# Attention and a mixture of experts on one core: first-row scores of two heads from a tile of their own

## The chip, the cores and the metric

One core of a Trainium2 chip runs the whole program. TensorE (PE in the views; PEld is its weight load), VectorE (DVE), ScalarE (ACT) and GpSimd (POOL) each work through a fixed list of instructions in order and wait for each other by semaphores; SyncE (SP) issues the DMAs. The metric is device time in microseconds (us) of one launch, the median of several runs.

## The reference

```
scores = scale * np.matmul(q, k.transpose(0, 1, 3, 2))      # (4, 8, 576, 64) each
bias = -(cum[:, :, :, None] - cum[:, :, None, :])           # cum: cumsum of max(s, 0)
scores = np.where(causal, -1e9, scores + np.minimum(bias, 0.0))
attn = softmax(scores);  x = attn @ v                       # -> (2304, 512)
for e in range(4):
    h = np.maximum(x @ w1[e], 0.0)                          # 512 -> 1024
    out += p[:, e:e + 1] * (h @ w2[e])
```

Everything is float32. Where a product needs more than one pass, the kernel splits an operand into a rounded part ("hi", type F32R) and the remainder ("lo") and adds products of the parts.

## The kernel before, in words

**Stages.** First comes attention over 32 heads. While it runs, TensorE also works through the first expert (group by group of token tiles, lines L888 and L901), which fills the places where attention has nothing ready. What is left of the first expert then runs alone, while GpSimd and the DMAs prepare the operands of the last stage. The last stage, experts 1 to 3, is a seven-product scheme (L1189 first layer, L1199 second layer).

**Order.** For the attention stage the class `Sched` plays the program on the host with cost estimates for each task: a task has the engines that may do it, a priority, the buffers that it takes and gives back, and the tasks that it depends on. The order in which this play starts the tasks is the order of the instructions on each engine of the chip. TensorE's filler is taken whenever no attention task is ready by the play's own clock. After that the chip's engines simply follow their lists.

**A visit.** The loop over `VISITS` handles one head at a time. The first eight heads come first, in two halves each; visits 16 to 39 are the other 24 heads, each with all 576 query rows at once, and the two heads of a neighbouring pair follow each other. For a head of these 24, q and k arrive as one `raw` tile [128, 576] (rows 0 to 63 are q, 64 to 127 are k, transposed). ACT or POOL makes the hi part, DVE or POOL the lo part, in the tile `AB`. Three DMAs build `KK` from it (L654 to L656; the last copies rows of the cumulated bias out of the DRAM tile `ce_d`), and two DMAs fill the second half of `AB` (L660, L661). A score tile is then two accumulating matmuls (L696): 128 rows deep, for the hi parts of q with hi and lo of k, and 68 deep, for the lo part of q and the bias rows. Behind it come a masked row minimum on DVE (L707), the exponential on ACT (L715), the normalisation (L430/L432), transposes on TensorE (L742) and the product with v (L793).

**The first 64 rows.** Rows 0 to 63 of a head see only 64 keys. The function `pair_rows` does them for two neighbouring heads in one softmax tile of 128 rows: head one in rows 0 to 63, head two in rows 64 to 127. Before the change its scores are four matmuls (L546), two for each head, each with 64 columns. Their weights are 128 columns of that head's `AB`, read from 64 columns further left for the second head, so that it lands in the lower rows; `AB` has 64 columns more for that, which GpSimd clears (L361). The first of the pair's visits so keeps its `AB` and `KK` until the second visit has its own. The v rows of the pair come in two small DMAs (L533) into `vraw0`. Later, L584 multiplies the pair's probabilities with its v.

**The weights' staging tiles.** `stage` is two tiles [128, 1024] through which the eight weight blocks of the first expert are loaded and split, early in attention.

Of the kernel before, what the change touches and what calls it, by code (L numbers as in the profile page):

```python
# [61 lines left out]
def t_act(n, psum=True):  # L62
    return n / 1.2 + (55 if psum else 95)
# [258 lines left out]

def body(ctx, tc, qk, vp, s, dp, w1, w1s, w2, w2s, out):
    nc = tc.nc
# [31 lines left out]

    def AB_raw(j, dt=F32R):
        fresh = late.get(tok["AB", j], (None, None))[0] != dt
        t = slot(tok["AB", j], [P, 64 + 2 * S], dt, apool)
        if fresh and dt == F32R:  # L360
            nc.gpsimd.memset(t[:, 0:64].bitcast(F32), 0.0)  # L361
        return t

    def AB(j, dt=F32R):
        return AB_raw(j, dt)[:, 64:].rearrange("p (x n) -> p x n", x=2)

# [36 lines left out]
    make("xh", 1, [P, 2, S])  # L403
    make("stage", 2, [P, 1024])
    make("osb", 2, [P, DM])
    make("mx", 8, [P, 2])
    make("sm", 8, [P, 1])
    make("vraw0", 1, [P, D])
    make("V0", 2, [P, P], F32R)
# [118 lines left out]

    def pair_rows(j, h, base, ready, last):
# [5 lines left out]
        v_hi = sch.add({"ACT": t_act(64, False), "POOL": (t_pool_hi(64), D2)}, lambda e: hi(e, tok["V0", k][:, 0:64], tok["vraw0", k]), [ldv],  # L535
                       prio=base - PV, take=[("V0", k)], seq="V0")
        v_lo = sch.add({"DVE": (t_dve(64), D7), "POOL": (t_pool2(64), 0)}, lambda e: sub(e, tok["V0", k][:, 64:P], tok["vraw0", k], tok["V0", k][:, 0:64].bitcast(F32)),
                       [v_hi], prio=base - PV, give=[("vraw0", k)])
# [58 lines left out]
    pair_deps = {}  # L597
    qk_before, last_before = [], None
    x_done = {}
# [4 lines left out]
    for j, (h, ms) in enumerate(VISITS):  # L604
# [3 lines left out]
        ext = rows(ms[-1])[1]  # L608
        q0 = rows(ms[0])[0]
        nb = ms[-1] + 1  # L610
        first = j < NH
# [30 lines left out]
        else:  # L642
            if pq:
                qk_ready = [ld, ldc]
            else:
                qk_hi = sch.add({"ACT": t_act(ext, False), "POOL": (t_pool_hi(ext), D2)}, lambda e, j=j, ext=ext: hi(
                    e, AB(j)[:, 0, 0:ext], tok["raw", j][:, 0:ext]), [ld], prio=base - PQ, take=[("AB", j)], seq="AB")
                qk_lo = sch.add({"DVE": (t_dve(ext), D7), "POOL": (t_pool2(ext), 0)}, lambda e, j=j, ext=ext: sub(
                    e, AB(j)[:, 1, 0:ext], tok["raw", j][:, 0:ext], AB(j)[:, 0, 0:ext].bitcast(F32)),
                    [qk_hi], prio=base - PQ, give=[("raw", j)])  # L650
                qk_lo.both = True

                def f(e, j=j, h=h, ext=ext):
# [5 lines left out]
                def f(e, j=j, h=h, ext=ext, q0=q0):  # L659
                    nc.sync.dma_start(out=AB(j)[64:128, 0, q0:ext].bitcast(F32), in_=AB(j)[0:64, 0, q0:ext].bitcast(F32))  # L660
                    nc.sync.dma_start(out=AB(j)[64:68, 1, q0:ext].bitcast(F32), in_=ced[h, 0:4, q0:ext])  # L661
                q_dma = sch.add({"SP": 1100}, f, [k_dma], prio=base - 1600, xfer=256 * (ext - q0))
                qk_ready = [k_dma, q_dma]
# [9 lines left out]
        last_q = None  # L673
        joint = ms == tuple(range(NC))
        if joint and o:
            pair_rows(j, h, base, qk_before + qk_ready, last_before)
        for m in ms[1:] if joint else ms:
# [7 lines left out]
            for pi, (j0, j1) in enumerate(pieces):  # L685
                lastp = pi == len(pieces) - 1

                def f(e, j=j, a=a, j0=j0, j1=j1, c=c, pi=pi, ext=ext, pq=pq, h=h):
# [8 lines left out]
                qt = sch.add({"PE": (t_pe4(j1 - j0) if pq else 2 * t_pe(j1 - j0))}, f, qk_ready + [last_q], prio=pr + pi, take=[("S", (c, pi))],  # L697
                             give=([("AB", j)] if pq else [("AB", j), ("KK", j)] if o or not joint else []) if lastp and m == ms[-1] else [])
                last_q = qt
# [163 lines left out]
    for which in (1, 2):  # L863
        for i in range(4):
            pr = (W1 if which == 1 else W2) + i
            k = (which, i)
            ld = sch.add({"SP": 500}, lambda e, k=k: load_w(0, k[0], k[1], tok["stage", k]), prio=pr - 5500 + WS, take=[("stage", k)], xfer=524288)
            n, lo = 1024 // WH, None
            for x in range(WH):
                c0, c1 = x * n, x * n + n  # L870
                hd = sch.add({"ACT": (t_act(n, False), DWA), "POOL": (t_pool_hi(n), DWQ)}, lambda e, k=k, c0=c0, c1=c1: hi(
                    e, w_tiles(*k)[0][:, c0:c1], tok["stage", k][:, c0:c1]), [ld, lo], prio=pr)
                lo = sch.add({"DVE": (t_dve(n), DWL), "POOL": (t_pool2(n), DWP)}, lambda e, k=k, c0=c0, c1=c1: sub(
                    e, w_tiles(*k)[1][:, c0:c1], tok["stage", k][:, c0:c1], w_tiles(*k)[0][:, c0:c1].bitcast(F32)),
                    [hd], prio=pr, give=[("stage", k)] if x == WH - 1 else [])
# [516 lines left out]
```

## Time and profile before

| | |
|---|---|
| median of 3 runs | 925.06 us (924.97 to 925.24) |
| profiled execution, own time | 925.23 us |
| its span, first to last instruction | 923.4 us |
| busy PE, PEld, DVE, ACT, POOL | 99%, 95%, 75%, 49%, 53% of the span |
| granted TensorE clock | 1.00 throughout |

The profile's times count from the span's start. The program spends 1.8 us of its own time outside the span. A busy figure is the time in which an engine has at least one instruction under way; matmuls overlap, so the pace of TensorE is read from the distance of starts and not from durations.

### The profile page before, as it was taken

The numbers are of one execution on the slowest core, as the hardware profiler recorded it, in microseconds if no ns is written. First come the engines' busy times: TensorE is split into PE (matmuls) and PEld (weight loads), VectorE is DVE, ScalarE is ACT, GpSimd is POOL, SyncE is SP. The second block draws the span as 40 slices with busy tenths as digits, with TensorE's granted clock in tenths as the row PEclk, the third lists the DMA queues.
The fourth block names the chain that finished last, engine by engine and source line by source line (L and its number), as shares of the span: only waits on it lengthen the run. The fifth ranks groups of instructions, "written<-read, shape, count | busy, mean of one in ns | idle before, by whom it ended". The sixth has DMA issues, their size and how long they took to land.

```text
span 923.4 us, 17444 instructions
## 1 busy us (share of the span) xinstructions
PE 916.6 (99%) x6127; PEld 876.0 (95%) x6127; DVE 689.8 (75%) x1655; ACT 453.7 (49%) x1034; POOL 487.5 (53%) x531
## 2 busy tenths in 40 slices
PE   9999999999999999999999999999999999999998
PEld 6789998998898998999999999999999999999998
DVE  7888888888851221577879797968796889678976
ACT  5799998998840110443335342525243433434240
POOL 5788787777726794222634362437144813572222
PEclk9999999999999999999999999999999999999999
DMA  5688778778427956296487546854587457754603
GB/s 156 199 257 231 209 209 228 218 208 240 137 90 244 361 199 231 81 364 217 153 281 245 178 146 242 283 192 140 197 283 230 143 192 246 240 182 143 218 25 121
DMA packets 126280, 188.39 MB, mean 204 GB/s; under 512 B 12352, under 2 KB 103520, under 8 KB 126192
## 3 DMA queue, kind: packets, MB, share of 16 engines
q1 hardware_dynamic: 126192, 187.26, 63.4%
q8 instruction: 49, 0.80, 0.3%
q14 instruction: 39, 0.32, 0.1%
HBM read 143.95 MB, written 29.02 MB: 187 GB/s over the span
## 4 chain that ended last, share of the span: by engine, by line
PE 94%; DVE 1%; ACT 1%; issue 1%; POOL 1%; DMA 1%; SPq 0%; DVEq 0%; POOLq 0%; ACTq 0%
PE pb L1189 26%; PE pb L1199 21%; PE mo L1199 8%; PE mo L888 7%; PE mo L901 6%; PE pv L793 5%; PE pb L901 5%; PE T L742 4%; PE pb L888 3%; PE S L696 3%; PE S L693 2%; PE X L742 1%; PE X L696 0%; DMA xf_d<-xr 0%; PE S L546 0%
## 5 line engine op out<-in xcount | busy, mean ns | idle before, releaser
L1189 PE MATMUL pb<-x,w1h 128*128 128x384 f32 x1008 | 256.7, 335 | 0.6 <-ACT t L1229 0.3
L1189 PEld LDWEIGHTS pb<-x,w1h 128*128 128x128 f32 x1008 | 180.8, 188 | 2.5 <-DVE t L1233 1.8
L424 POOL TENSOR_TENSOR hT_r<-t,hT_r 128x768 fp32r<-128x768 f32 x18 | 33.9, 1883 | 268.6 <-PE pb L1189 215.6
L1189 PE MATMUL pb<-x,w1l 128*128 128x384 f32 x504 | 168.5, 334 | 0.0
L1229 ACT ACTIVATE t<-pb 128x384 f32<-128x384 f32 x144 | 66.4, 486 | 160.8 <-PE pb L1189 151.6
L1292 DVE SCALAR_TENSOR_TENSOR acc<-pb,prob,acc 128x256 f32<-128x256 f32 x288 | 125.9, 473 | 5.3 <-PE pb L1199 4.9
L1199 PE MATMUL pb<-w2h,hT_r 128*128 128x256 f32 x720 | 114.6, 283 | 0.1
L1199 PEld LDWEIGHTS pb<-w2h,hT_r 128*128 128x128 f32 x720 | 99.6, 191 | 0.3 <-issue 0.3
L1233 DVE TENSOR_TENSOR t<-pb,t 128x384 f32<-128x384 f32 x108 | 54.4, 549 | 57.6 <-PE pb L1189 36.1
L1189 PEld LDWEIGHTS pb<-x,w1l 128*128 128x128 f32 x504 | 94.6, 188 | 0.0
L1206 ACT ACTIVATE hT_r<-t 128x768 fp32r<-128x768 f32 x54 | 45.7, 846 | 98.2 <-PE pb L1199 92.7
L1203 DVE SCALAR_TENSOR_TENSOR t<-t 128x768 f32<-128x768 f32 x72 | 88.0, 1222 | 1.7 <-issue 1.6
L715 ACT ACTIVATE a<-a,mx 128x448 f32<-128x448 f32 (+4 forms) x136 | 81.1, 598 | 13.6 <-DVE mx L707 12.6
L888 PE MATMUL mo<-xg,w1h 128*128 128x384 f32 (+1 forms) x320 | 80.1, 323 | 0.0
L432 POOL TENSOR_SCALAR a<-a,sm 128x192 f32<-128x192 f32 (+5 forms) x107 | 60.8, 572 | 31.9 <-DVE sm L723 18.2
L1199 PE MATMUL pb<-w2l,hT_r 128*128 128x256 f32 x360 | 71.5, 283 | 0.0
L1292 DVE SCALAR_TENSOR_TENSOR acc<-mo,prob,acc 128x256 f32<-128x256 f32 x144 | 62.7, 473 | 1.6 <-PE mo L1199 1.6
L1203 DVE SCALAR_TENSOR_TENSOR hT_r<-t,hT_r 128x768 fp32r<-128x768 f32 x54 | 56.8, 1053 | 7.6 <-ACT hT_r L1206 7.1
L707 DVE CUSTOM_DVE_ANT_0 a<-S,mask 128x288 f32<-128x288 f32 (+4 forms) x115 | 51.9, 461 | 10.8 <-PE S L693 5.2
L771 DVE TENSOR_TENSOR aTl<-T,aTh 128x256 fp32r<-128x256 f32 (+2 forms) x104 | 51.4, 500 | 9.5 <-ACT aTh L437 8.6
L888 PEld LDWEIGHTS mo<-xg,w1h 128*128 128x128 f32 x320 | 55.2, 189 | 1.2 <-issue 0.6
L1199 PEld LDWEIGHTS pb<-w2l,hT_r 128*128 128x128 f32 x360 | 55.7, 192 | 0.0
(188 smaller groups left out, 2163.7 us busy)
## 6 DMA issues: line engine op xcount, KB each, us to landing
x<-xs_d SPq DMA_DIRECT2D x68, 768.0 KB
x<-x_d SPq DMA_DIRECT2D x55, 768.0 KB
xs_d<-x SPq DMA_DIRECT2D x12, 768.0 KB
raw<-in_qk_dram SPq DMA_DIRECT2D x24, 288.0 KB
KK<-AB_r SPq DMA_DIRECT2D x24, 288.0 KB
x_d<-xh SPq DMA_DIRECT2D x12, 576.0 KB
xg<-x_d SPq DMA_DIRECT2D x16, 384.0 KB
w1r<-in_w1s_dram SPq DMA_DIRECT2D x6, 1024.0 KB
```

Of the source, the lines that this page charges most:

```text
L432: (nc.gpsimd if e == "POOL" else nc.vector).tensor_scalar(out, in_, scale, 1.0 if bias is None else bias, op0=ALU.mult, op1=ALU.mult if bi ...
L707: nc.vector.tensor_tensor_reduce(out=z[0:n, j0:j1], in0=tok["S", (c, pi)][0:n, 0:j1 - j0], in1=mask[0:n, 448 - a + j0:448 - a + j1], scale ...
L715: nc.scalar.activation(z[0:n, 0:bb], z[0:n, 0:bb], AF.Exp, bias=tok["mx", c][0:n, k:k + 1], scale=-1.0, accum_out=tok["sm", c][0:n])
L771: nc.vector.tensor_tensor(out=dst, in0=src, in1=h_.bitcast(F32), op=ALU.subtract)
L888: nc.tensor.matmul(t[:, 0:w], wl[q][:, dc, o:o + P], xgt[:, l, dc, 0:w], start=(u == 0), stop=(u == 3 * KD - 1))
L901: nc.tensor.matmul(t, ht[:, fc, 128 * ti:128 * ti + 128], wl[fc // 2][:, fc % 2, :], start=(u == 0), stop=(u == 3 * KF - 1))
L1189: nc.tensor.matmul(ts[u][:, 0:TG], wv[wl][:, k, 128 * u:128 * u + 128], x[:, xl_, k, :], start=start and k == 0 and n == 0, stop=k == 1 an ...
L1199: nc.tensor.matmul(ts[t][:, 0:256], h_part(o, hl_)[:, k, 128 * t:128 * t + 128], wv[wl][:, k, :], start=start and k == 0 and n == 0, stop= ...
L1203: (nc.gpsimd if e == "POOL" else nc.vector).scalar_tensor_tensor(out=out, in0=in0, scalar=0.0, in1=in1, op0=ALU.max, op1=op)
L1229: nc.scalar.activation(tmp[name][:, u], ts[u][:, 0:TG], f)
L1233: nc.vector.tensor_tensor(out=tmp[name][:, u], in0=ts[u][:, 0:TG], in1=tmp[name][:, u], op=ALU.add)
L1292: nc.vector.scalar_tensor_tensor(out=a_, in0=ts[t][:, 0:256], scalar=prob[:, tt, e:e + 1], in1=a_, op0=ALU.mult, op1=ALU.add)
```

## The change

The pair's scores no longer use the tiles of the two heads. Each pair gets one DMA from a new input, `qkv0`, that the host has laid out: for each pair 128 rows of q and k of the first 64 positions of both heads (128 columns of q, 128 of k, the 64 rows given twice) and 64 columns of v. It goes into one of two slots in `stage0`. ACT or POOL writes the hi part of all 256 columns, DVE or POOL the lo part, ACT or POOL then writes the hi part of k over 64 rows of the lo part, and two DMAs copy the bias rows of both heads. These parts lie in halves of `stage1`. The scores are then two matmuls with 128 columns, whose blocks of one head's rows with the other's keys the mask already excludes. The staging tiles are used by pairs only after all eight weight blocks have been split. `AB` loses its 64 cleared columns, the first head's `AB` and `KK` are given back after its own visit, and the `AB` copies of these visits start at column 64.

```
-        ldv = sch.add({"SP": 700}, lambda e: [nc.sync.dma_start(out=tok["vraw0", k][64 * x:64 * x + 64], in_=vp[h - 1 + x][0:64, 0]) for x in range(2)],
-                      [firstq.get(j - LV)], prio=base - 1290, take=[("vraw0", k)], seq="vraw0", xfer=128 * 64 * 4)
+        def f(e):
+            r = 320 * tok["praw", k]
+            nc.sync.dma_start(out=slot("stage0", [P, 1024], F32, apool)[:, r:r + 320], in_=qkv0[(h - NH) // 2])
+        ld = sch.add({"SP": 500}, f, [firstq.get(j - LA)], prio=base - 1500, take=[("praw", k)], xfer=320 * P * 4)
+        pair_loads.append(ld)
...
+        p_hi = sch.add({"ACT": t_act(256, False), "POOL": (t_pool_hi(256), D2)}, lambda e: hi(e, pair_tile(k)[1], pair_tile(k)[0]), [ld], prio=base - PQ,
+                       take=[("pqk", k)])
+
+        p_lo = sch.add({"DVE": (t_dve(256), D7), "POOL": (t_pool2(256), 0)}, lambda e: sub(e, pair_tile(k)[2], pair_tile(k)[0], pair_tile(k)[1].bitcast(F32)),
+                       [p_hi], prio=base - PQ)
+        p_lo.both = True
+        p_cp = sch.add({"ACT": t_act(P, False), "POOL": (t_pool_hi(P), D2)}, lambda e: hi(e, pair_tile(k)[2][0:64, P:], pair_tile(k)[0][0:64, P:]), [p_lo], prio=base - PQ)
+
+        def f(e):
+            for t, c in ((pair_tile(k)[2][64:68, 0:P], 0), (pair_tile(k)[1][64:68, P:], 2)):
+                nc.sync.dma_start(out=t.bitcast(F32).rearrange("p (y n) -> p y n", y=2), in_=ced[h - 1:h + 1, c:c + 4, 0:64].rearrange("y r n -> r y n"))
+        p_ce = sch.add({"SP": 900}, f, [p_lo, t_ced], prio=base - 1600, xfer=4096)
 
         def f(e):
             t = tok["S", (k, "p")]
-            for y, i in enumerate((j - 1, j)):
-                for x, n in ((0, P), (1, 68)):
-                    q = AB_raw(i)[0:n, 64 + S * x - 64 * y:64 + S * x - 64 * y + P]
-                    nc.tensor.matmul(t[:, 64 * y:64 * y + 64], q, tok["KK", i][0:n, x, 0:64], start=(x == 0), stop=(x == 1))
-        qt = sch.add({"PE": 4 * t_pe(64)}, f, ready + [last], prio=pr, take=[("S", (k, "p"))], give=[("AB", j - 1), ("KK", j - 1)])
-        firstq.setdefault(j, qt)
+            _, (q0, k1), (q1, k0) = (x if i == 0 else (x[:, 0:P], x[:, P:]) for i, x in enumerate(pair_tile(k)))
+            nc.tensor.matmul(t[:, 0:P], q0, k0, start=True, stop=False)
+            nc.tensor.matmul(t[:, 0:P], q1[0:68], k1[0:68], start=False, stop=True)
+        qt = sch.add({"PE": 2 * t_pe(P)}, f, [p_cp, p_ce, v_lo], prio=pr, take=[("S", (k, "p"))], give=[("praw", k), ("pqk", k)])
+        qt.lag = S_LAG
...
-                    nc.sync.dma_start(out=AB(j)[64:68, 1, q0:ext].bitcast(F32), in_=ced[h, 0:4, q0:ext])
+                    nc.sync.dma_start(out=AB(j)[64:68, 1, qs:ext].bitcast(F32), in_=ced[h, 0:4, qs:ext])
...
+            for t in pair_loads:
+                lo.next.append(t)
+                t.wait += 1
```

The two orders show where the new instructions stand. On TensorE, before the change, the first pair's four matmuls (`S<-KK,AB_r`, L546) stand between transposes (L742) behind filler (L901):

```order
L901 MATMUL mo_1_104<-w2h0_85,hT1_r_615 128x512 x2
L742 MATMUL T_0_99<-idn_74,a1_0_122 128x128 x2
L546 MATMUL S_1_98<-KK_1_112,AB0_r_771 128x64 x2
L546 MATMUL S_1_98<-KK_2_113,AB1_r_884 128x64 x2
L742 MATMUL X_0_102<-idn_74,a2_0_124 128x128 x3
L742 MATMUL T_1_100<-idn_74,a3_0_126 128x128 x4
```

With the change the first pair's two matmuls (L567 and L568, from `stage1`; the transposes are now L765, the head's own scores L719, the filler L926) stand at the same place in the program:

```order
L765 MATMUL T_0_99<-idn_74,a2_0_124 128x128 x3
L765 MATMUL X_0_102<-idn_74,a3_0_126 128x128 x4
L567 MATMUL S_0_97<-stage1_r_979 128x128
L568 MATMUL S_0_97<-stage1_r_979 128x128
L765 MATMUL T_1_100<-idn_74,a4_0_128 128x128 x2
L719 MATMUL S_1_98<-KK_2_113,AB1_r_880 128x288 x2
L926 MATMUL mo_1_104<-w2h3_88,hT1_r_614 128x512 x2
```

Four matmuls of 64 columns became two of 128; neighbours changed a little because the host's play ran differently. Over the whole program the counts of all other TensorE instructions are the same in both orders, the warm-up matmuls included; 15 more of the filler matmuls of L888 (now L913) stand ahead of the last attention matmul, and 15 fewer behind it.

On SyncE's list, where all DMAs are issued in order, the stretch of the first two pairs before the change has the v rows (L533, two DMAs) among the copies for `KK` and `AB`:

```order
L656 DMA KK_2_113<-ce_d_159 4x576
L628 DMA raw_1_106<-in_qk_dram 128x576
L630 DMA vraw_0_114<-in_vp_dram 128x320
L533 DMA vraw0_0_154<-in_vp_dram 64x64 x2
L654 DMA KK_0_111<-AB2_r_961 64x2x576
L655 DMA KK_0_111<-AB2_r_961 64x576
L656 DMA KK_0_111<-ce_d_159 4x576
L660 DMA AB1_r_884<-AB1_r_884 64x576
L661 DMA AB1_r_884<-ce_d_159 4x576
```

With the change the bias rows of a pair (L561, two DMAs from `ce_d`) stand there (`AB` copies are now L684 and L685, `KK` copies L678 to L680; the pair's load, L543, stands some 20 rows earlier):

```order
L685 DMA AB1_r_880<-ce_d_158 4x512
L866 DMA x_d_159<-xh_0_133 128x2x256
L906 DMA xg_93<-x_d_159 128x2x256 x2
L561 DMA stage1_r_979<-ce_d_158 4x2x64 x2
L654 DMA vraw_1_115<-in_vp_dram 128x320
L684 DMA AB2_r_925<-AB2_r_925 64x512
L685 DMA AB2_r_925<-ce_d_158 4x512
L906 DMA xg_93<-x_d_159 128x2x256
L561 DMA stage1_r_979<-ce_d_158 4x2x64 x2
```

Each pair has three DMAs in place of two, and two of them wait for the pair's lo part, with the next head's copies queued behind them.

## Rows read from the trace of the kernel before

**Rows 1.** Page: busy us of each engine; chain that ended last.

```profile
PE 916.6 (99%) x6127; PEld 876.0 (95%) x6127; DVE 689.8 (75%) x1655; ACT 453.7 (49%) x1034; POOL 487.5 (53%) x531
...
PE 94%; DVE 1%; ACT 1%; issue 1%; POOL 1%; DMA 1%; SPq 0%; DVEq 0%; POOLq 0%; ACTq 0%
```

**Rows 2.** Stretches: length, busy PE, PEld, DVE, ACT, POOL, clock, DMA.

```profile
0.00:75.00 75.00, 73.01 (x460) 60.05 (x461) 61.04 (x257) 57.41 (x172) 52.43 (x97) 1.00 0.71 202
75.00:270.00 195.00, 194.75 (x1293) 179.86 (x1292) 161.54 (x615) 173.39 (x478) 145.45 (x267) 1.00 0.70 200
270.00:382.00 112.00, 112.00 (x597) 101.68 (x596) 26.65 (x47) 17.58 (x38) 70.28 (x47) 1.00 0.64 222
```

**Rows 3.** Waits of PE and PEld, 75 to 270 us: total, times, longest.

```profile
PE T L742 <- DVE aTl L771: 0.2, 1, 0.2
...
PEld T L742 <- issue: 0.7, 2, 0.5
PEld S L696 <- DVE mx L707: 0.7, 3, 0.3
PEld pv L793 <- DVE xr L808: 0.3, 1, 0.3
```

**Rows 4.** Line L546: duration ns min/median/max, first and last start us, forms.

```profile
L546 PE MATMUL S<-KK,AB_r x40: 192/277/298, 77.6 to 247.3; 128*128 128x64 f32 x20, 68*128 68x64 f32 x20
...
L546 PE MATMUL X<-KK,AB_r x8: 194/277/277, 106.0 to 183.1; 128*128 128x64 f32 x4, 68*128 68x64 f32 x4
```

**Rows 5.** Timeline of PE and of PEld at two pairs: start, length, count.

```profile
120.95 0.61 PE L546 MATMUL S<-KK,AB_r 128*128 128x64 f32 x4
121.39 0.45 PE L696 MATMUL X<-KK,AB_r 128*128 128x192 f32 x2
121.68 0.43 PE L888 MATMUL mo<-xg,w1h 128*128 128x256 f32 x2
...
131.99 0.52 PEld L546 LDWEIGHTS S<-KK,AB_r 128*128 128x128 f32 x4
132.46 0.20 PEld L742 LDWEIGHTS X<-idn,a 128*128 128x128 f32 x2
```

**Rows 6.** Timeline of PE: pairs of matmuls with 128 columns (L584).

```profile
129.58 0.37 PE L584 MATMUL X<-aT,V 128*128 128x128 f32 x2
129.79 0.33 PE L888 MATMUL mo<-xg,w1l 128*128 128x256 f32 x1
...
269.88 0.33 PE L584 MATMUL X<-aT,V 128*128 128x128 f32 x2
270.05 0.39 PE L888 MATMUL mo<-xg,w1h 128*128 128x384 f32 x1
```

**Rows 7.** ACT and POOL groups, 75 to 270 us: count, busy us, mean ns.

```profile
L437 ACT ACTIVATE AB_r<-raw 128x576 fp32r<-128x576 f32 x12 | 8.2, 684 | 0.0
...
L430 ACT ACTIVATE a<-a,sm 128x576 f32<-128x576 f32 x7 | 5.4, 771 | 0.5 <-DVE sm L723 0.5
...
L437 ACT ACTIVATE V<-vraw 128x320 fp32r<-128x320 f32 x11 | 5.1, 468 | 0.8 <-PE pv L793 0.8
...
L437 ACT ACTIVATE V<-vraw 128x64 fp32r<-128x64 f32 x2 | 0.5, 257 | 0.8 <-PE T L584 0.8
...
L424 POOL TENSOR_TENSOR V<-vraw,V 128x320 fp32r<-128x320 f32 x24 | 21.1, 879 | 0.4
...
L424 POOL TENSOR_TENSOR V<-vraw,V 128x64 fp32r<-128x64 f32 x11 | 3.6, 325 | 0.6
```

**Rows 8.** SyncE: issue ns of two lines; one of its waits, 75 to 270 us.

```profile
L533 SPq DMA_DIRECT2D vraw<-in_vp_dram x24: 488/587/894, 58.0 to 229.5; - x24
...
L661 SPq DMA_DIRECT2D AB_r<-ce_d x24: 424/483/879, 63.3 to 238.2; - x24
...
SPq L655 <- POOL sm L721: 3.0, 7, 0.6
```

**Rows 9.** First and last start of the last stage's matmuls; GpSimd's last sum.

```profile
L1189 PE MATMUL pb<-x,w1h x1008: 333/334/446, 382.6 to 888.4; 128*128 128x384 f32 x168
...
355.58 1.85 POOL L424 TENSOR_TENSOR x<-t,x 128x768 fp32r<-128x768 f32 x1
```

More of the change, by code (lines that the diff above doesn't have):

```diff
@@ L320, in run, with body @@
                 now = min(later)
-def body(ctx, tc, qk, vp, s, dp, w1, w1s, w2, w2s, out):
+def body(ctx, tc, qk, qkv0, vp, s, dp, w1, w1s, w2, w2s, out):
     nc = tc.nc
@@ L355, in hT, with stage_tile, pair_tile @@
         return slot(f"hT{l}", [P, KF, TG], F32R)
[L357 to L362, printed above, removed]
-    def AB(j, dt=F32R):
-        return AB_raw(j, dt)[:, 64:].rearrange("p (x n) -> p x n", x=2)
+    def AB(j, dt=F32R):
+        return slot(tok["AB", j], [P, 2 * S], dt, apool).rearrange("p (x n) -> p x n", x=2)
+    def stage_tile(k):
+        return slot(tok["stage", k], [P, 1024], F32, apool)
+    def pair_tile(k):
+        r, c = 320 * tok["praw", k], 512 * tok["pqk", k]
+        t = slot("stage1", [P, 1024], F32R, apool)
+        return slot("stage0", [P, 1024], F32, apool)[:, r:r + 256], t[:, c:c + 256], t[:, c + 256:c + 512]
     pattn = actx.enter_context(tc.tile_pool(name="psa", bufs=1, space=PSUM))
@@ L403, in body @@
     make("xh", 1, [P, 2, S])
-    make("stage", 2, [P, 1024])
+    sch.pool("stage", [f"stage{i}" for i in range(2)])
+    sch.pool("praw", range(2))
+    sch.pool("pqk", range(2))
+    for i in range(2):
+        slot(f"stage{i}", [P, 1024], F32, apool)
     make("osb", 2, [P, DM])
@@ L407, in body @@
     make("sm", 8, [P, 1])
-    make("vraw0", 1, [P, D])
     make("V0", 2, [P, P], F32R)
@@ L526, in body, with pair_rows, v_raw @@
     t_prob = sch.add({"DVE": 500}, emit_dp, [t_dpl], prio=8000, take=[("S", "dp"), ("mx", "dp")], give=[("S", "dp"), ("mx", "dp"), ("osb", "dp")])
-    def pair_rows(j, h, base, ready, last):
+    def pair_rows(j, h, base):
         k = j // 2
         pr = base
-        ldv = sch.add({"SP": 700}, lambda e: [nc.sync.dma_start(out=tok["vraw0", k][64 * x:64 * x + 64], in_=vp[h - 1 + x][0:64, 0]) for x in range(2)],
-                      [firstq.get(j - LV)], prio=base - 1290, take=[("vraw0", k)], seq="vraw0", xfer=128 * 64 * 4)
-        v_hi = sch.add({"ACT": t_act(64, False), "POOL": (t_pool_hi(64), D2)}, lambda e: hi(e, tok["V0", k][:, 0:64], tok["vraw0", k]), [ldv],
+        def v_raw():
+            r = 320 * tok["praw", k] + 256
+            return slot("stage0", [P, 1024], F32, apool)[:, r:r + 64]
+        def f(e):
[3 more added lines that the diff above has]
+        pair_loads.append(ld)
+        v_hi = sch.add({"ACT": t_act(64, False), "POOL": (t_pool_hi(64), D2)}, lambda e: hi(e, tok["V0", k][:, 0:64], v_raw()), [ld],
@@ L536, in pair_rows @@
                        prio=base - PV, take=[("V0", k)], seq="V0")
-        v_lo = sch.add({"DVE": (t_dve(64), D7), "POOL": (t_pool2(64), 0)}, lambda e: sub(e, tok["V0", k][:, 64:P], tok["vraw0", k], tok["V0", k][:, 0:64].bitcast(F32)),
-                       [v_hi], prio=base - PV, give=[("vraw0", k)])
+        v_lo = sch.add({"DVE": (t_dve(64), D7), "POOL": (t_pool2(64), 0)}, lambda e: sub(e, tok["V0", k][:, 64:P], v_raw(), tok["V0", k][:, 0:64].bitcast(F32)),
+                       [v_hi], prio=base - PV)
@@ L597, in body @@
     pair_deps = {}
-    qk_before, last_before = [], None
+    pair_loads = []
     x_done = {}
@@ L609, in body @@
         q0 = rows(ms[0])[0]
+        joint = ms == tuple(range(NC))
+        qs = 64 if joint else q0
         nb = ms[-1] + 1
@@ L673, in body @@
         last_q = None
-        joint = ms == tuple(range(NC))
         if joint and o:
-            pair_rows(j, h, base, qk_before + qk_ready, last_before)
+            pair_rows(j, h, base)
         for m in ms[1:] if joint else ms:
@@ L697, in body @@
                 qt = sch.add({"PE": (t_pe4(j1 - j0) if pq else 2 * t_pe(j1 - j0))}, f, qk_ready + [last_q], prio=pr + pi, take=[("S", (c, pi))],
-                             give=([("AB", j)] if pq else [("AB", j), ("KK", j)] if o or not joint else []) if lastp and m == ms[-1] else [])
+                             give=([("AB", j)] if pq else [("AB", j), ("KK", j)]) if lastp and m == ms[-1] else [])
                 last_q = qt
@@ L866, in body @@
             k = (which, i)
-            ld = sch.add({"SP": 500}, lambda e, k=k: load_w(0, k[0], k[1], tok["stage", k]), prio=pr - 5500 + WS, take=[("stage", k)], xfer=524288)
+            ld = sch.add({"SP": 500}, lambda e, k=k: load_w(0, k[0], k[1], stage_tile(k)), prio=pr - 5500 + WS, take=[("stage", k)], xfer=524288)
             n, lo = 1024 // WH, None
```

18 lines of the change are left out of this document (10 added, 8 removed).

## The prediction, made before the changed kernel ran

> **What bounds the kernel now.** I read the page first: TensorE is busy 99% of the span and the chain that ended last is 94% TensorE [rows 1]. That figure alone says little, since overlapping matmuls look busy even where one starts late, so the next view was the table of stretches [rows 2]. Attention with these pairs lies between 75 and 270 us. There TensorE shows 194.75 of 195 us, because the first expert's matmuls fill what attention leaves open; from 270 to 382 us it has no gap at all. The list of its waits between 75 and 270 us confirms it: 0.2 us on TensorE and 0.7, 0.7 and 0.3 us on its weight loads, 1.9 us together, none of them for a DMA [rows 3]. So in these stages time is TensorE's own work, and an instruction that is taken out of its list shortens the program by the time from its start to the next one's, if nothing new is waited for.
>
> The other engines are full but not to the brim in that stretch: ACT 173.4, DVE 161.5, POOL 145.5 of 195 us [rows 2]. That is where the change adds work.
>
> Whether a gain at 270 us reaches the end is seen from what follows. The last stage's first matmul starts at 382.6 us, while GpSimd's last operand sum starts at 355.58 us and lasts 1.85 us [rows 9]. That is 25 us of cover, so the last stage begins when TensorE is through with the first expert, and all behind it moves with TensorE.
>
> **What the change takes away on TensorE.** There are 48 matmuls of 64 columns in the trace (40 into one bank's name, 8 into another), four for each of 12 pairs [rows 4]. Their mean durations, near 277 ns, are latency; their price is the distance of starts. One set of four starts at 120.95 us, and the next instruction at 121.39: 0.44 us. The weight loads of another set start at 131.99 us, and the next load at 132.46: 0.47 us [rows 5]. I take 0.45 us for a set, 0.1125 us for one matmul.
>
> What two of 128 columns cost is not in the trace for these operands. The nearest rows are the two matmuls of L584, also 128 columns and weights of 128 columns: 129.58 to 129.79 us, and 269.88 to 270.05, so 0.21 and 0.17 us for two [rows 6]. They use the same weights twice, which could make them cheap. On the other side stands a pair of score matmuls of 192 columns with the same depths of 128 and 68 rows, as in the new pair: 121.39 to 121.68 us, 0.29 us for two [rows 5]. So two cost between 0.17 and 0.29 us. I take 0.225, two of the four steps: the columns that stream through are 256 in both versions, but the weight loads in rows 5 follow each other at 0.12 us whatever the 64 columns need, and the change has half as many. A set then saves 0.45 - 0.225 = 0.225 us, and 12 sets save 2.7 us. With the ends of the bounds it is 12 x (0.44 - 0.29) = 1.8 us at least, 12 x (0.47 - 0.17) = 3.6 us at most.
>
> One rule of the Trainium skill speaks against this. "TensorE: Matmul & The Clock Gate", section "Back-to-back issue gap", gives the gap of a single matmul by its columns, some 60 cycles up to 64 columns and 134 for 128; as an estimate by that page, four cost 100 ns, two 112 ns, and the change would lose a little. The same page's section on LDWEIGHTS has the load cost the weight columns divided by 1.2 GHz, 107 ns for 128; as an estimate, four loads cost 0.43 us and two 0.21. The trace agrees with the second, at 0.44 to 0.47 us for four [rows 5].
>
> The 15 filler matmuls that move ahead of attention's end cost nothing, since they are 15 fewer behind it, on the same engine.
>
> **What it adds elsewhere.** Counted over the two orders of ACT, its work grows by 6 splits of `AB` (0.684 us each), 9 of the new hi parts with 256 columns and 10 of the 128-column writes, less 4 normalisations of 576 columns (0.771 us), with the rest near nothing. The new shapes lie between 257 ns for 64 columns and 468 ns for 320 [rows 7]; by the slope between these, 0.415 us for 256 and 0.31 for 128. That is 4.1 + 3.7 + 3.1 - 3.1 = 7.8 us more on 173.4 of 195 us. ACT still has 13.8 us without work there, so its cover is that idle time; without cover it would be up to 7.8 us on the path. POOL gets 9 lo parts of 256 columns, between 325 ns for 64 and 879 for 320 [rows 7], by the slope 0.74 us each, 6.7 us; it gives 6 `AB` splits to ACT and takes 4 normalisations from it, and its idle time is 49 us. DVE gets three lo parts, a little over 1 us, with 33 us idle. All of it stands in lists that leave TensorE's filler in between.
>
> On SyncE the pair's two v loads of 0.587 us issue time go, and come one load and two copies of bias rows; the nearest are the copies of L661 with 0.483 us [rows 8], so 3 x 0.48 - 2 x 0.587, some 0.3 us more for each pair of about 15 us. Packets of 16 DMA engines are under way 0.70 of the time [rows 2], and the new bytes are 164 KB for 32 KB in a pair, less the shorter `AB` copies: under 0.1 of the 3 MB that 15 us move at 200 GB/s. What is queued behind the new copies on SyncE are the next head's `KK` and `AB` copies, and TensorE's next scores wait for those. The trace shows no wait of TensorE for such copies now [rows 3], though the same queue does wait for POOL, up to 0.6 us at a time at L655 [rows 8].
>
> GpSimd no longer clears the 64 columns; that was off the path.
>
> **Sum.** The profiled execution took 925.23 us of its own time, 0.17 above the median of the runs. From the median: 925.06 - 2.7 = 922.4 us. For what the new order does to TensorE's waits I take nothing: it may lose some of the 1.9 us that are there, or add as many.
>
> **Rivals.** A measurement of this kernel can tell about 0.2%, 1.85 us, from no change.
>
> *The gain is given back in the same stretch (about the same).* ACT with 181 of 195 us has less room to catch up, and a transpose, a product or a score that TensorE has in its list at a fixed place comes late. New waits of 0.85 us are enough to bring the gain under 1.85 us; if the 1.9 us of rows 3 double, the time is 925.06 - 2.7 + 1.9 = 924.3 us. For it: ACT was the fullest of the helpers. Against: with 89% busy it caused none of the waits of rows 3. 18%.
>
> *Columns set the price (the same).* Then two matmuls with the 256 columns of the four take the same 0.45 us, nothing is saved, and the time is 925.1 us. Against it: two matmuls of 192 columns, half as many columns again as the new ones, took 0.29 us [rows 5], and two of 128 took 0.17 and 0.21 [rows 6]. 2%. The skill's page "TensorE: Matmul & The Clock Gate", section "Back-to-back issue gap", is the rule that such a result would follow; its section on LDWEIGHTS speaks for the forecast.
>
> *The new copies are late (slower).* The second of the two matmuls (L568) needs the bias rows, which SyncE issues only after the pair's lo part is done, behind everything else in its list; TensorE can pass nothing around it. It decides from 0.225 us of wait per pair, and the kernel is slower by 1.85 us from 0.38 us per pair. With 0.6 us per pair, the longest wait of SyncE at L655, it is 925.06 - 2.7 + 7.2 = 929.6 us. Against it: 24 heads already wait for copies of the same kind (L661), and no wait of TensorE for a DMA is listed. 8%.
>
> *More than the weight loads (faster still).* The first head of a pair no longer keeps `AB` and `KK` until its neighbour is ready, so copies can start sooner; if most of the 1.9 us of waits go too, 925.06 - 2.7 - 1.4 = 921.0 us. But none of those waits names a copy. 10%.
>
> **Numbers.** The forecast, about 921.6 to 923.2 us, has 62%, and the predicted time is 922.4 us. Faster by over 0.2% holds it and the last rival, 72%; within 0.2% 20%; slower 8%. The range for 8 in 10 goes down to 925.06 - 3.6 - 0.6 = 920.9 us (the largest saving and a third of the waits) and up to 925.06 - 1.8 + 1.5 = 924.8 us (the smallest saving and three quarters of another 1.9 us of waits).
>
> **What would show it.** Right: 24 matmuls of L567 and L568 with 0.2 to 0.24 us from a pair's first start to the next instruction; waits of TensorE between 75 and 270 us near 2 us in sum; the last stage's first matmul near 379.9 us instead of 382.6; from there to the end the same length as before; ACT busier by some 8 us before 270 us. Wrong: waits of TensorE at L568 for a DMA, or a list of waits for ACT or POOL that has grown by more than 1 us, or a pair of two that still takes 0.3 us and more.

## The result, and the profile after

The changed kernel is slower: a median of 930.88 us (930.32 to 931.56, 6 runs) against 925.17 us (924.97 to 925.59, 6 runs) on the same chip, a ratio of 1.0061 with a 95% interval of 1.0050 to 1.0072. The prediction was 922.4 us, with a range from 920.9 to 924.8 and 8% for slower.

The page of the changed kernel, and the table of stretches with the columns of [rows 2]:

```profile
PE 918.0 (99%) x6103; PEld 874.0 (94%) x6103; DVE 689.5 (74%) x1661; ACT 459.0 (49%) x1057; POOL 492.1 (53%) x534
```

```profile
75.00:270.00 195.00, 194.57 (x1274) 177.50 (x1273) 161.74 (x618) 177.31 (x497) 151.14 (x274) 1.00 0.71 203
270.00:300.00 30.00, 30.00 (x154) 27.16 (x153) 6.74 (x12) 4.55 (x10) 11.52 (x8) 1.00 0.46 163
300.00:345.00 45.00, 44.59 (x233) 41.29 (x233) 9.59 (x17) 6.89 (x14) 39.34 (x27) 1.00 0.87 308
345.00:375.00 30.00, 27.23 (x146) 23.57 (x146) 4.84 (x9) 2.24 (x6) 16.58 (x12) 0.94 0.59 202
```

In the stretch with the pairs ACT has grown by 3.9 us and POOL by 5.7 us, and TensorE's column has hardly moved. (The 7.8 us that were forecast for ACT are a sum of durations; the busy column counts the time in which ACT's instructions overlap once.) The last row is where the time is lost: TensorE, without a gap before [rows 2], has 27.23 of 30 us, and its granted clock is 0.94. The last stage starts at 388.2 us for 382.6 [rows 9], which is the whole loss:

```profile
L1214 PE MATMUL pb<-x,w1h x1008: 333/335/446, 388.2 to 894.0; 128*128 128x384 f32 x168
```

To see where along the way, I compare starts at a fixed place in TensorE's list. With the pairs' score matmuls left out, both lists have 6079 matmuls, and up to the 1801st they hold the same ones, all of attention among them. That one starts at 289.81 us before and 289.42 after: attention gave 0.39 us and not 2.7. The 2201st starts at 365.56 and 371.18: the tail behind attention took 6.0 us. Each start is read from one execution; how far that carries is said at the table of the experiments.

**What TensorE waits for in the tail.** The list of waits from 300 to 385 us, and its timeline at the longest:

```profile
PEld pb L913 <- DMA xg<-x_d: 4.5, 5, 2.8
PE pb L913 <- DMA xg<-x_d: 2.8, 2, 2.4
```

```profile
363.06 0.51 PE L913 MATMUL pb<-xg,w1h 128*128 128x256 f32 x2 [2.42 <-DMA xg<-x_d]
...
367.81 0.63 PE L913 MATMUL pb<-xg,w1h 128*128 128x256 f32 x2
...
368.45 0.63 PE L913 MATMUL mo<-xg,w1h 128*128 128x256 f32 x2
...
369.39 0.40 PE L913 MATMUL mo<-xg,w1h 128*128 128x256 f32 x2
...
369.75 0.40 PE L913 MATMUL mo<-xg,w1h 128*128 128x256 f32 x2
```

```profile
355.00:362.00 7.00, 5.64 (x25) 4.33 (x24) 1.50 (x2) 0.00 (x0) 6.75 (x5) 1.00 0.65 187
362.00:365.20 3.20, 1.86 (x9) 1.25 (x9) 0.00 (x0) 0.00 (x0) 0.26 (x1) 1.00 1.09 378
365.20:368.90 3.70, 3.62 (x18) 3.62 (x19) 0.42 (x1) 0.60 (x2) 0.00 (x0) 0.55 1.07 395
368.90:375.00 6.10, 6.10 (x52) 6.10 (x52) 1.70 (x4) 1.65 (x5) 0.00 (x0) 0.99 0.39 146
```

The wait is for `xg`, the first expert's input tiles, which SyncE copies from `x_d`. The pause costs twice: in the table of stretches the granted clock is 0.55 for the 3.7 us behind it, near the lower of its two levels (1.2 of 2.4 GHz), and three matmuls of 256 columns take 0.64 us (367.81 to 368.45) for 0.36 a little later (369.39 to 369.75). That is some 3.7 x 0.45 = 1.7 us beside the 4.5 us of waits, as an estimate, together near the 6.0 us that the tail took.

**Why `xg` is late.** SyncE's own queue (SPq: start, length, count), before and then after, where the first sum's operands are loaded and where the last `xg` copies stand:

```profile
277.01 0.88 SPq L1009 DMA_DIRECT2D t<-xf_d  x2
277.94 2.01 SPq L881 DMA_DIRECT2D xg<-x_d  x4
279.99 2.12 SPq L1009 DMA_DIRECT2D t<-xf_d  x2
...
331.60 21.56 SPq L1026 DMA_DIRECT2D xs_d<-x  x4
353.25 2.82 SPq L881 DMA_DIRECT2D xg<-x_d  x4
```

```profile
279.03 0.37 SPq L1034 DMA_DIRECT2D t<-xf_d  x1
279.45 2.37 SPq L906 DMA_DIRECT2D xg<-x_d  x4
281.87 2.31 SPq L1034 DMA_DIRECT2D t<-xf_d  x3
...
336.54 21.51 SPq L1051 DMA_DIRECT2D xs_d<-x  x4
358.14 2.80 SPq L906 DMA_DIRECT2D xg<-x_d  x4
```

In both kernels the last four `xg` copies stand behind four stores of GpSimd's sums (`xs_d`), and these wait for GpSimd over 21.5 us. And before, two raw operands of the first sum were loaded ahead of four `xg` copies; after, one is, and the second comes behind. GpSimd's first sum needs both (timeline of POOL, before and after):

```profile
281.36 1.84 POOL L993 TENSOR_TENSOR t<-t 128x768 f32<-128x768 f32 x1 [7.84 <-DMA t<-xf_d]
```

```profile
289.58 1.83 POOL L1018 TENSOR_TENSOR t<-t 128x768 f32<-128x768 f32 x1 [13.55 <-DMA t<-xf_d]
```

It starts 8.2 us later; the stores and the last `xg` copies follow 4.9 us later (358.14 for 353.25). The order has this from the code: the steps behind attention are placed by `spent`, the TensorE work that has been put into the list since attention ended. The first raw load has the mark 0.0, the second 2.0 us. With the 15 filler matmuls taken ahead of attention, a group's `xg` copies come up before the mark of 2.0 is reached.

**Attention itself.** A new pair, and its two lines:

```profile
119.34 0.31 PE L567 MATMUL S<-stage_r 128*128 128x128 f32 x1
119.48 0.28 PE L568 MATMUL S<-stage_r 68*128 68x128 f32 x1
119.59 0.34 PE L913 MATMUL mo<-xg,w1h 128*128 128x256 f32 x1
```

```profile
L567 PE MATMUL S<-stage_r x11: 221/246/309, 81.7 to 244.2; 128*128 128x128 f32 x11
L567 PE MATMUL X<-stage_r x1: 222/222/222, 107.9 to 107.9; 128*128 128x128 f32 x1
```

This pair takes 0.25 us to the next start. Over all 12 the distances sum to 2.67 us, 0.22 a pair, where the 48 matmuls took 4.98: TensorE's list is shorter by 2.31 us. No wait stands at L567 or L568. The waits of the weight load between 75 and 270 us have grown from 1.7 us in sum [rows 3] to about 5, in many small ones, of which the largest are:

```profile
PEld T L606 <- DVE aTl L794: 0.8, 3, 0.3
PEld T L765 <- POOL sm L744: 0.6, 2, 0.4
PEld T L765 <- DVE aTl L794: 0.6, 2, 0.4
PEld T L765 <- issue: 0.5, 2, 0.3
PEld S L719 <- DVE mx L730: 0.5, 2, 0.3
PEld T L765 <- POOL a L436: 0.4, 1, 0.4
PEld X L765 <- POOL V L428: 0.4, 1, 0.4
```

Those that name ACT or POOL, of which [rows 3] had none, sum to 1.8 us, nearly all of it POOL. The prediction had named such a growth, by more than 1 us, as a sign of being wrong.

### The profile page after: what moved, and what is told of

Same layout as the page of the kernel before. It is cut to its first block, busy times and chain, and to the rows that moved or that the text cites. A ratio compares the mean times of both kernels' runs of the same rounds, so it can differ in the third digit from the quotient of the medians.

```text
span 929.1 us, 17461 instructions
## 1 busy us (share of the span) xinstructions
PE 918.0 (99%) x6103; PEld 874.0 (94%) x6103; DVE 689.5 (74%) x1661; ACT 459.0 (49%) x1057; POOL 492.1 (53%) x534
## 4 chain that ended last, share of the span: by engine, by line
PE 93%; DMA 2%; DVE 2%; issue 1%; POOL 1%; ACT 1%; SPq 0%; DVEq 0%; POOLq 0%; ACTq 0%
PE pb L1214 26%; PE pb L1224 21%; PE mo L1224 8%; PE mo L913 8%; PE mo L926 6%; PE pv L815 5%; PE pb L926 4%; PE T L765 4%; PE S L719 3%; PE pb L913 3%; PE S L716 2%; PE X L765 1%; DMA xg<-x_d 1%; PE X L719 1%; PE X L716 0%
## 5 line engine op out<-in xcount | busy, mean ns | idle before, releaser
L913 PE MATMUL mo<-xg,w1h 128*128 128x384 f32 (+1 forms) x328 | 84.3, 328 | 0.0
L436 POOL TENSOR_SCALAR a<-a,sm 128x448 f32<-128x448 f32 (+5 forms) x109 | 62.5, 579 | 23.4 <-DVE sm L746 10.0
L913 PEld LDWEIGHTS mo<-xg,w1h 128*128 128x128 f32 x328 | 57.4, 190 | 1.4 <-issue 0.6
L730 DVE CUSTOM_DVE_ANT_0 a<-S,mask 128x320 f32<-128x320 f32 (+4 forms) x112 | 50.8, 463 | 9.9 <-PE S L716 5.3
L765 PE MATMUL T<-idn,a 128*128 128x128 f32 x333 | 55.7, 275 | 0.9 <-POOL a L436 0.5
```

The costliest lines, as they stand in the source:

```text
L436: (nc.gpsimd if e == "POOL" else nc.vector).tensor_scalar(out, in_, scale, 1.0 if bias is None else bias, op0=ALU.mult, op1=ALU.mult if bi ...
L765: nc.tensor.transpose(t[:, 128 * k:128 * k + 128], z[:, 128 * x:128 * x + 128], idn)
L913: nc.tensor.matmul(t[:, 0:w], wl[q][:, dc, o:o + P], xgt[:, l, dc, 0:w], start=(u == 0), stop=(u == 3 * KD - 1))
```

## The experiments

Two questions were tried apart: what the tail loses, and why attention keeps so little of 2.31 us. Each expectation says in its own words what its theories are; a letter there only numbers them. In the table the two columns at the right are the starts of the 1801st and of the 2201st TensorE matmul (pairs' scores left out) against 289.81 and 365.56 us. The ratio is to the kernel before on the same chip, with its 95% interval; beside the median stands its difference from that kernel's median there, in brackets.

A start comes from a single execution. The first four rows have the same attention, instruction for instruction on TensorE, ACT, DVE and POOL, and their 1801st starts lie within 0.3 us. But before_raws_late has the attention of the kernel before, in the same order, and its start is 1.31 us later: its profiled execution took 929.09 us, 1.45 more than its median. That of light_act_four took 1.0 us more than its median, and that of before_two128 0.6 us less. So the medians are read beside the starts.

| run | median us | ratio | 1801st | 2201st |
|---|---|---|---|---|
| changed kernel | 930.88 (+5.71) | 1.0061 (1.0050 to 1.0072) | -0.39 | +5.62 |
| raws_first | 925.62 (-0.14) | 0.9996 (0.9987 to 1.0006) | -0.23 | +0.34 |
| stores_last | 925.98 (+0.22) | 1.0005 (0.9996 to 1.0015) | -0.09 | +1.18 |
| best_tail | 924.75 (-0.53) | 0.9994 (0.9985 to 1.0004) | -0.38 | -0.37 |
| before_raws_late | 927.64 (+1.88) | 1.0020 (1.0010 to 1.0029) | +1.31 | +3.86 |
| before_two128 | 925.45 (-0.31) | 0.9996 (0.9987 to 1.0006) | -0.54 | -0.54 |
| before_eight | 928.79 (+3.51) | 1.0038 (1.0023 to 1.0053) | +3.69 | +3.69 |
| light_pairs | 923.69 (-1.59) | 0.9984 (0.9975 to 0.9993) | -2.11 | -1.13 |
| heavy_pairs | 931.17 (+5.89) | 1.0064 (1.0047 to 1.0081) | +5.35 | +5.81 |
| light_act | 923.58 (-1.77) | 0.9981 (0.9971 to 0.9990) | -2.20 | -1.40 |
| light_copies | 926.10 (+0.75) | 1.0010 (1.0001 to 1.0019) | -0.51 | +1.52 |
| copy_on_pool | 924.57 (-0.78) | 0.9992 (0.9982 to 1.0001) | -0.77 | -0.77 |
| both_sooner | 925.78 (+0.43) | 1.0006 (0.9997 to 1.0015) | +0.55 | +0.55 |
| before_light | 925.08 (-0.32) | 0.9996 (0.9986 to 1.0005) | -0.21 | -0.21 |
| two128_light | 923.68 (-1.72) | 0.9982 (0.9972 to 0.9991) | -1.54 | -1.54 |
| light_act_four | 924.33 (-1.07) | 0.9991 (0.9982 to 1.0000) | -1.04 | +0.26 |

### The tail

**raws_first**: the changed kernel with both raw loads ahead again. The marks are those of two groups of sums, so the second group's second load moves up as well, ahead of two loads of weights.

```
-        for at, part in zip(... else (0.0, 2.0, T_LOAD, T_LOAD + 2.0), order):
+        for at, part in zip(... else (0.0, 0.0, T_LOAD, T_LOAD + 2.0), order):
```

> The changed kernel, with both loads of raw operands that GpSimd's first sum needs issued before the four xg copies, as in the kernel before. Theory A (the loss is behind attention: on SyncE's list one of these loads fell behind the xg copies, GpSimd's sums and their stores all come some 5 us late, and the last xg copies behind the stores with them): GpSimd's first sum starts at 281 to 285 us instead of 289.6, the waits of TensorE for xg between 320 and 370 us (7.3 us listed) shrink to under 1.5 us, and the time is 925.0 to 926.5 us. Theory B (the loss is in attention, from fuller ACT, POOL and SyncE lists): no change, 930 to 931.5 us.

The median fell by 5.3 us from the changed kernel's. GpSimd's first sum starts 4.8 us sooner, the last `xg` copies 5.3 us (352.83 for 358.14); of the waits for `xg` 0.2 us on TensorE and 0.4 us on its weight load are left:

```profile
284.74 1.84 POOL L1018 TENSOR_TENSOR t<-t 128x768 f32<-128x768 f32 x1 [8.55 <-DMA t<-xf_d]
```

```profile
331.22 21.52 SPq L1051 DMA_DIRECT2D xs_d<-x  x4
352.83 2.82 SPq L906 DMA_DIRECT2D xg<-x_d  x4
```

**stores_last**: the changed kernel with the raw loads as they are, and the stores of the last group's sums moved behind the `xg` copies. **best_tail** has both edits.

```
-            yield now, lambda o=o: store(o)
+            yield now + (60.0 if held is not None else 0.0), lambda o=o: store(o)
```

> The changed kernel, with the four stores of the last group's sums issued behind the last xg copies instead of ahead of them; GpSimd's sums stay late. Theory A: the last xg copies start near 346 us instead of 358, the wait at 363 us and the lower clock behind it vanish, the 0.7 us wait at 328 us stays, time 925.3 to 926.5 us. Theory B: no change, 930 to 931.5 us.

> The changed kernel with both edits behind attention: the second raw load ahead of the xg copies, and the four last stores behind the last xg copies. Theory A: no wait of TensorE for xg is left (0.6 us less than raws_first), so 924.8 to 925.4 us; it is 0.3 us or so below the kernel before.

In stores_last GpSimd's first sum is still late (290.12 us), but the last `xg` copies no longer wait for it, and most of the loss is gone:

```profile
336.98 0.36 SPq L1051 DMA_DIRECT2D xs_d<-x  x1
343.62 1.92 SPq L906 DMA_DIRECT2D xg<-x_d  x4
348.85 9.65 SPq L1051 DMA_DIRECT2D xs_d<-x  x3
```

With both edits no wait for `xg` is listed at all, and the tail neither gains nor loses (-0.38 at its start, -0.37 behind it). What the change is worth without the loss is then 0.5 us by the medians, with 1 still in its interval.

**before_raws_late**: the kernel before, whose second raw load gets the mark 4.0 for 2.0.

> The kernel before, with one edit: the second raw load is issued behind the xg copies, as the changed kernel has it by its planner. Attention is untouched. Theory A: GpSimd's first sum starts near 287 us, the last xg copies come 3 to 5 us later than before, and the kernel loses 2 to 5 us: 927 to 930 us. Theory B: nothing is lost, 925.2 us.

The order of SyncE's list becomes that of the changed kernel, in a kernel with the old pairs, and the tail loses too: 2.6 us (from +1.31 to +3.86), and 1.9 us by the medians:

```profile
278.12 0.37 SPq L1009 DMA_DIRECT2D t<-xf_d  x1
278.54 2.10 SPq L881 DMA_DIRECT2D xg<-x_d  x4
280.68 1.77 SPq L1009 DMA_DIRECT2D t<-xf_d  x3
...
357.90 2.80 SPq L881 DMA_DIRECT2D xg<-x_d  x4
```

It is less than the 6.0 us of the changed kernel. Here the last copies start 66.8 us behind the 1801st matmul, there 68.7; and here the granted clock stays at 1.00 through the tail, where the lower clock cost there some 1.7 us by the estimate above. What the profiled execution lost in attention (1.31 us, there by its first 1200 matmuls) its edit does not explain.

### Attention

**before_two128**: the kernel before with two matmuls of 128 columns in place of the four, in the same order. Both come from the second head's tiles; the first head's 64 rows of scores are left out. **before_eight**: each of the four issued twice.

```
-            for y, i in enumerate((j - 1, j)):
...
+            for x, n in ((0, P), (1, 68)):
+                q = AB_raw(j)[0:n, S * x:S * x + P]
+                nc.tensor.matmul(t[:, 0:P], q, tok["KK", j][0:n, x, 0:P], start=(x == 0), stop=(x == 1))
```

```
-            for y, i in enumerate((j - 1, j)):
+            for y, i in list(enumerate((j - 1, j))) * 2:
```

> The kernel before, in which the pair's scores are two matmuls of 128 columns from the second head's own tiles, in the same order of all instructions; it leaves out the first head's 64 rows of scores. It prices the matmuls by themselves. Half the weight loads, half the price: TensorE is 2.7 us ahead at the end of attention and the time is 922.3 to 923.5 us, if the waits behind attention don't grow by what TensorE gains. Columns set the price: 925.2 us.

> The kernel before, with each pair's four matmuls issued twice (48 more, 0.1125 us each by the rows, 5.4 us of TensorE's list). Theory C (in attention TensorE meets its neighbours at many places; what it gains or loses between two of them is mostly taken up by short late starts that the list of waits doesn't show): it costs clearly less than 5.4 us, 1 to 3.5 us, so 926.5 to 929.3 us. Theory D (TensorE alone sets attention's length, and in the changed kernel other work took the gain): the full 5.4 us, 931 us.

The pairs' distances fell from 4.98 to 2.86 us, and 0.54 of these 2.12 us arrived (0.31 by the medians). Twice the matmuls, 5.26 us more by their distances (10.24 in sum), cost 3.69 (3.51 by the medians), near the upper end of what theory C expected. TensorE's time counts in part, and less in the direction of a gain.

**light_pairs** leaves out the pair's hi and lo parts, its 128-column write and its bias copies in ten of the twelve pairs of raws_first; **heavy_pairs** makes the hi part and the 128-column write twice in all.

```
-        p_hi = ... lambda e: hi(e, pair_tile(k)[1], pair_tile(k)[0]), [ld], ...
+        p_hi = ... lambda e: hi(e, pair_tile(k)[1], pair_tile(k)[0]) if k < 10 else None, [ld], ...
...
```

```
-        p_hi = ... lambda e: hi(e, pair_tile(k)[1], pair_tile(k)[0]), [ld], ...
+        p_hi = ... lambda e: [hi(e, pair_tile(k)[1], pair_tile(k)[0]) for _ in range(2)], [ld], ...
...
```

> The raws_first kernel, in which ACT, POOL, DVE and SyncE make the pair's hi and lo parts and bias copies for the first two pairs only, and the other ten pairs reuse them; it leaves out that work, so scores of ten pairs are of other heads. Theory D: the added work cost what the matmuls gained, and without it the time falls by 1.5 to 2.3 us below raws_first, to 923.3 to 924.2 us. Theory C: 0 to 1 us below raws_first, since the matmuls' gain was not on the path.

> The raws_first kernel with the pair's hi part and its 128-column copy each made twice, 5.6 us more on ACT and 1.8 us more on POOL. Theory D: added work on ACT costs about what it takes, so 1.5 us or more above raws_first. Theory C: under 1 us above raws_first.

Without the pair's preparation attention ends 1.9 us sooner than in raws_first; with 8.6 us more of it by durations (6.8 on ACT, 1.8 on POOL) 5.6 us later. Both are what theory D expected: the added work costs time.

**light_act** and **light_copies** take that apart, on raws_first: the first leaves out only the hi part and the 128-column write in ten pairs, the second only the bias copies.

```
+        p_hi = ... hi(e, pair_tile(k)[1], pair_tile(k)[0]) if k < 10 else None, [ld], ...
...
+        p_cp = ... hi(e, pair_tile(k)[2][0:64, P:], pair_tile(k)[0][0:64, P:]) if k < 10 else None, [p_lo], ...
```

```
+            for t, c in (...) if k < 10 else ():
```

> Kernel raws_first, in which ten of the twelve pairs do not make the hi part of the 256 columns and not the 128-column write on ACT or GpSimd (that work is left out; the lo part, the two bias copies and the matmuls stay, with old data in the tile). Theory that the pair's ACT work stands on the path: most of the 2 us that light_pairs gained come back, so 923.6 to 924.2 us, and attention's matmuls end 1.2 to 2 us earlier than in raws_first. Rival, that the lo part and the two copies on SyncE's list cost the time: within 0.5 us of raws_first, 925.2 to 926.0 us.

> Kernel raws_first, in which ten of the twelve pairs do not copy their bias rows (two DMAs of SyncE less in each; that work is left out, all else stays). Theory that ACT's work stands on the path: within 0.5 us of raws_first, 925.2 to 926.0 us. Rival, that the copies hold up the next head's copies in SyncE's list: 923.6 to 924.4 us, with attention's end 1.2 to 2 us earlier.

The hi part and the 128-column write are it, 7.2 us of ACT and POOL together by durations (5.7 and 1.5): without them the 1801st matmul comes 1.97 us sooner, without the copies 0.3. light_pairs, which leaves out the lo parts and the copies too, came no further (-2.11 against -2.20), so the lo parts cost attention nothing, although POOL is 5.3 us less busy without them. Which of the two engines the cost comes from, and whether from its load or from the place of the writes in its list, these runs do not tell. (Behind attention light_copies met the wait for `xg` again, 1.2 us on TensorE, so its median does not show this.) The stretch from 75 to 270 us of raws_first, and then of light_act:

```profile
75.00:270.00 195.00, 194.52 (x1272) 177.14 (x1271) 161.66 (x618) 177.58 (x497) 151.62 (x274) 1.00 0.72 203
```

```profile
75.00:270.00 195.00, 194.92 (x1285) 179.33 (x1284) 162.26 (x620) 174.76 (x483) 149.58 (x270) 1.00 0.71 203
```

Busy TensorE differs by 0.40 us while its 1801st matmul differs by 1.97; busy PEld differs by 2.19 us, and the count of matmuls by 13.

**before_light, two128_light, light_act_four.** Then the same saving on TensorE with and without a relieved ACT. In the kernel before, and in before_two128, ten pairs leave out three short ACT instructions (the hi part of the transposed probabilities and two moves of the product); light_act_four is light_act with each of the two matmuls issued twice.

```
+        eh = ... lambda e: hi(e, tok["aT0", k][:, 0], tok["T", (k, "p")][:, 0:P]) if k < 10 else None, [tt], ...
...
+            sh = ... AF.Copy) if k < 10 else None, ...
```

```
+            for _ in range(2):
                 nc.tensor.matmul(t[:, 0:P], q0, k0, start=True, stop=False)
                 nc.tensor.matmul(t[:, 0:P], q1[0:68], k1[0:68], start=False, stop=True)
```

> Kernel before with its four matmuls, in which ten of the twelve pairs leave out three short ACT instructions (0.277 us and two of 0.219, 7.2 us in all): the hi part of the pair's transposed probabilities and the two moves of its product; that work is left out, the order stays. If ACT's list sets attention's end: 1 to 3 us below before, 922.3 to 924.3 us. If ACT has room, as my prediction took it: 0 to 0.5 us below, 924.8 to 925.4 us.

> The same three ACT instructions left out of before_two128 (two matmuls of 128 columns for the four, one head's scores left out). If ACT's load is what kept the saving of 2.1 us from counting: 1.6 to 2.2 us below before_light, 920.5 to 922.7 us. If the order of the lists does: 0.3 to 0.8 us below before_light, as before_two128 stood to before.

> Kernel light_act (the pair's hi part and 128-column write left out in ten pairs) with each of the pair's two matmuls issued twice, so that TensorE has back the 2.3 us that the change saves. If TensorE sets attention's end once ACT is relieved: 1.8 to 2.4 us above light_act, 925.4 to 926.0 us. If not: 0.3 to 0.8 us above, 923.9 to 924.4 us.

before_light came out as if ACT had room, 0.3 us under before. two128_light is 1.40 us below it, between the two expectations. light_act_four is 0.75 us above light_act, in the range for a TensorE that does not set attention's end even then, with 1.16 us at the 1801st matmul. At the 1801st matmul, in the kernel before: TensorE relieved alone -0.54 us, ACT relieved alone -0.21 (although ACT is 6.0 us less busy, the row below, against [rows 2]), both -1.54. By the medians they are -0.31, -0.32 and -1.72, each ratio with an interval of some 0.9 us to either side. With ACT relieved the saving counts 1.33 of 2.12 us, without 0.54; in the changed kernel the added matmuls (2.55 us by their distances) cost 1.16.

```profile
75.00:270.00 195.00, 194.57 (x1295) 180.28 (x1295) 161.60 (x616) 167.39 (x451) 144.91 (x267) 1.00 0.71 200
```

**copy_on_pool** and **both_sooner** are complete kernels on best_tail that let the play shift the new work from ACT to GpSimd: the first lets GpSimd have the 128-column write unless it is 1.2 us late by the play, the second takes GpSimd for both new writes already when ACT is 0.3 us late.

```
+        p_cp = sch.add({"ACT": (t_act(P, False), D2), "POOL": t_pool_hi(P)}, ...
```

```
+        p_hi = sch.add({"ACT": t_act(256, False), "POOL": (t_pool_hi(256), 300)}, ...
...
+        p_cp = sch.add({"ACT": t_act(P, False), "POOL": (t_pool_hi(P), 300)}, ...
```

> Kernel best_tail, complete, but the 128-column write prefers GpSimd, and ACT only when that is 1.2 us late by the play; ACT loses up to 3 us of work in attention, GpSimd has 50 us idle there. If ACT's work alone stands on the path: 923.0 to 924.0 us, the fastest complete kernel. If GpSimd's idle time covers no more than ACT's did: 924.5 to 925.8 us, as best_tail.

> Kernel best_tail, complete, but GpSimd takes the pair's hi part and its 128-column write already when ACT is 0.3 us late by the play, where it was 1.2 us. If ACT's work alone stands on the path: 923.0 to 924.2 us. If not: 924.5 to 925.8 us.

Both lie where they were expected if ACT's work alone is not on the path. copy_on_pool is the fastest complete kernel, 0.8 us below before, but its interval still holds 1; and ACT is no less busy in it between 75 and 270 us than in best_tail (177.89 for 177.41), since the play gave ACT other work. both_sooner is 1.2 us slower than that with ACT 2.3 us less busy (175.60): where the play puts things moves attention's end by about a microsecond either way.

## Why the prediction was wrong

**Right: what the operations cost.** Two of 128 columns take 0.22 us (0.225 forecast), a set of four took 0.415 (0.45 forecast), and the 12 sets save 2.31 us (2.7 forecast, within its bounds of 1.8 and 3.6). The rival that columns set the price is out. So is the rival of the late copies: no wait at L568, and light_copies gave 0.3 us. By the Trainium skill, "TensorE: Matmul & The Clock Gate", section on LDWEIGHTS, two loads of 128 columns cost 0.21 us as an estimate, and the trace agrees with 0.22. The prediction's other estimate by that page, from the table under "Back-to-back issue gap", that four of 64 are no dearer than two of 128, does not hold here, with 4.98 against 2.67 us; the section itself says that the figures are those of a single matmul and leave out the weight load.

**Wrong, and the cause of the sign: "That is 25 us of cover, so the last stage begins when TensorE is through with the first expert".** The prediction checked GpSimd's last sum against the last stage. GpSimd's earlier sums have a nearer user: their stores stand in SyncE's list ahead of the last `xg` copies, and TensorE needs these for what is left of the first expert. There the cover was nearly nothing. "The 15 filler matmuls that move ahead of attention's end cost nothing" fell with it: on TensorE they cost nothing, but the steps behind attention are placed by them. This took 6.0 us. That the order causes it is shown by raws_first, in which 5.4 of the 6.0 us are gone, and from the other side by before_raws_late, which loses 2.6 us in its profile and 1.9 by the medians; that the stores pass the delay on, by stores_last. The order of SyncE's list was to be had before the run; the prediction had read it only around the pairs.

**Wrong: "an instruction that is taken out of its list shortens the program by the time from its start to the next one's, if nothing new is waited for".** That took a TensorE busy for 194.75 of 195 us as the only limit. Of 2.12 us taken out in the order of before 0.54 arrived. The busy figure cannot tell: overlapping matmuls fill it even where weight loads start late, and between raws_first and light_act it moved by a fifth of the difference in progress. The Trainium skill, "Perfetto Trace Analysis", section "Identifying the Most-Contended Engine", says that matmul busy time is a poor measure of how far TensorE is from its limit, and names the busy share of the weight loads, beside the share of peak FLOPs, as what to use instead. The rows here agree: PEld was at 179.86 of 195 us [rows 2], and between raws_first and light_act it moved with the progress.

**Wrong: "ACT still has 13.8 us without work there, so its cover is that idle time".** The forecast of 0.415 and 0.31 us for the new writes was right (they took 0.413 and 0.304), and light_act shows that those on ACT and POOL together cost attention 2.0 us. Idle time spread over the stretch did not cover it. But the load of ACT alone is not shown to be the reason: in the kernel before, 6.0 us less of it gained 0.2 us.

So the change traded 2.3 us on TensorE for new work on ACT and POOL, in a stretch in which, by the four kernels with the old order, both sides limit together: one relieved gains 0.2 to 0.5 us, both 1.5 to 1.7. That is a reading of small differences and not as firm as that of the tail. The rival "given back in the same stretch" had this right for attention, and put 18% on it.

**What stays open.** light_act has helpers about as busy as before (ACT 455.3 for 453.7 us over the span) and the two matmuls, and its attention ends 2.20 us sooner; before_two128 has the same, and ends 0.54 sooner. What differs is the order on all engines and the tiles that come free sooner; the runs do not tell these apart. Nor does a run move the new writes to another place in ACT's list and leave its load as it is, which would tell the load from the place.

## What to carry to other kernels

A list with two engines' work in it passes delays on: for each queue look for the nearest user of what stands behind a waiting entry, not for the last. When an edit shifts filler past a stage's end, compare the order of the DMA queue behind that stage too, above all where steps are placed by work done. And where TensorE is filled up to 99% by work that was put into its gaps, take something off each engine in turn before pricing an edit by one of them.

## What was not expected of the hardware

A pause of 2.42 us for a DMA (TensorE was busy for 5.64 of the 7.0 us in which it began and for 1.86 of the next 3.2) was followed by 3.7 us at a granted clock of 0.55. As an estimate, the clock added some 1.7 us to waits of 4.5 us. In light_copies a pause of 1.19 us at the same place (5.82 of 7.0 us, then 3.10 of 3.2) was followed by a granted clock of 1.00.
